# One key block for the plain heads' last 64 queries, and the last 64 tokens' second token product made for two batches at once

## The chip, the core and the metric

The kernel runs on one core of a Trainium2 chip, as one launch. The metric is the device time of that launch in microseconds (us). Three runs of the kernel before the change took 294.07, 294.44 and 294.89 us; the median, 294.44 us, is the time before.

## What is computed

Eight batches of 576 tokens go through attention with 8 heads of 64 channels and then through a mixer. Cut to what matters here:

```python
scores = q @ k.T / sqrt(64)
rel = query_position - key_position
plain  (heads 0..3): keys with 0 <= rel < 32
dilated (heads 4..7): keys with 0 <= rel < 128 and rel % 4 == 0
x = softmax(scores, masked) @ v          # [8, 576, 512], heads side by side
h = relu(x.T @ w_tok1) @ w_tok2          # token mixing: 576 -> 256 -> 576
u = x + h.T
out = u + relu(u @ w_ch1) @ w_ch2        # channel mixing: 512 -> 1536 -> 512
```

A plain head's query sees the 32 keys that end at its own position, so queries 512 to 575 see keys 481 to 575 and no others. A dilated head's query looks back 127 positions.

## The kernel before, in words

**Tokens.** A batch's 576 tokens are four blocks of 128 (`s` = 0 to 3) and a tail of 64 (`s` = 4). Two batches share one 128-row tile for their tails: the even batch has rows 0 to 63, the odd one rows 64 to 127 (`u16t`, `gta[:, :, 512:640]`), so the channel stage does both tails at once, in the odd batch's stage.

**Attention.** Head pairs `hp` 0 and 1 are plain, 2 and 3 dilated. Keys, transposed, are in `kt[hp]`, 640 columns: 0 to 511, then the 64 tail keys, then 64 zeros. Scores are made keys by queries, exponentials go to fp16 tiles (`attp`, `attd`; the tails' to `attt`), and a mask is multiplied in on POOL (`mult`, L112), or, for batches 0 and 1, added on PE as one more matmul per block (`veil`, L390). Batches 0 to 2 make scores with 128-row matmuls (L392); from batch 3 on `scores_twin` (L465 on, matmuls on L475) gives each head of a pair one half of the array's rows. The tail queries of every head are scored against two key blocks, columns 384 to 511 and 512 to 639 of `kt`. `values` (L543 on) multiplies the exponentials with the values `vv` (a column of ones gives the sum): for a plain head seven matmuls for the four blocks (L552, L554) and two for the tail (L562, L564), all of 65 columns. DVE takes the reciprocal (L567) and scales into `xn` (L112).

**Mixer.** `emit_h1` (L570 on) makes the hidden token layer in two column halves and two row halves `jb`, five matmuls each (L576, L578), and a relu moves it to the tile `h1`. `emit_u` (L581 on) multiplies with `w_tok2` and adds `xn` on DVE. For the tail (`s` = 4) it makes the product of 128 weight columns with `h1` (2 matmuls of 512 columns, L601), of which only 64 rows of the result are read: zeros or other tokens' columns fill the rest. For batch 0 the same is written out in `u_half` (L886 on), in halves of 256 columns. `gen_main` (L652 on) is a batch's channel stage: `gp` (L716) and, in odd batches, `gt` (L707) for the tails, then `yp` (L735, and L755 for the tails).

**The order of work.** Instructions run in the order written; `interleave` (L763 on) decides it. It walks through a batch's channel stage (`gen_main(b)`), whose pieces have costs, and puts in a step of the attention and mixing of the following batches as soon as the sum of the costs reaches the step's due time. So stage `b` carries the values and mixing of batch `b+1` (`mix_steps`, L677 on, with due times for the two halves of `h1`, for `u` and for its transposes), and scores, casts, DMA transposes and the copies behind them (`place_steps`, L360 on, on POOL) of batch `b+2`, and loads of batch `b+3`. In steps of stages 2 to 6, `h1` is due at 5.4. Psum banks come from pools: `fl` (three) serves `av`, `h1p`, `up` and, in turn with the others, scores; `sc` has two, `main` three. A bank is written again when its reader is done, and a matmul that needs one waits on the reader's engine.

**Before the first stage** batch 0's attention and mixing run alone, while POOL issues the weight loads in between its casts. POOL then waits for the first channel weights (`gate`, L803) before the loads of batch 1 are let go.

## Time and profile before

| what | value |
|---|---|
| median of the three runs | 294.44 us (294.07 to 294.89) |
| the profiled execution's own span | 293.5 us, 7087 instructions |
| PE, matmul | 279.5 us busy (95%), 2850 matmuls |
| PE, weight load | 214.4 us (73%) |
| DVE | 132.6 us (45%) |
| ACT | 134.4 us (46%) |
| POOL | 165.3 us (56%) |
| granted clock of PE | full in all 40 slices |
| DMA | 52.12 MB, mean 178 GB/s |

The span runs from the first to the last instruction of one profiled execution; a run's time holds about 0.9 us more than it (294.44 - 293.5). An instruction's duration is from its start to its own end. Matmuls are pipelined, so one starts long before the one ahead of it has ended: what a matmul costs PE is the step from its start to the next start, not its duration. L12 is line 12 of the kernel before.

### The profile page before, as it was taken

Reading aid. Unit: us, or ns where it says so; the run is one execution under the profiler, and the core shown is the slowest. Engines: PE = TensorE matmul, PEld = TensorE weight load, DVE = VectorE, ACT = ScalarE, POOL = GpSimd, SP = SyncE. Lnnn points to the kernel's source line nnn. Section 1 sums busy time; section 2 is a strip of 40 time slices with the busy share of each in tenths; the row PEclk is TensorE's granted clock in tenths of the full one; section 3 lists DMA queues with packets and bytes.
Section 4 is the critical chain, followed back from the end, with each engine's and each line's share of the span. In section 5 each row is a group of like instructions: output and inputs, shape, how many; then the busy total and the mean of one; then the engine's idle time right before and its main releaser. Section 6 shows DMA issues by size and latency. Waiting matters only on the chain.

```text
span 293.5 us, 7087 instructions
## 1 busy us (share of the span) xinstructions
PE 279.5 (95%) x2850; PEld 214.4 (73%) x2850; DVE 132.6 (45%) x279; ACT 134.4 (46%) x266; POOL 165.3 (56%) x227
## 2 busy tenths in 40 slices
PE   5899889998999999999999999999999999999994
PEld 2796576796766796689766886698776976896593
DVE  6576658443844218422841246415640264422022
ACT  2774562237554534465346704482346625224500
POOL 5972463225999399929972899369952930000000
PEclk9999999999999999999999999999999999999999
DMA  7998999965899986859995999289874320431032
GB/s 219 269 195 178 288 231 235 256 159 169 271 246 175 308 233 168 123 105 318 254 206 108 304 235 236 56 192 334 211 143 91 93 71 2 88 112 36 2 88 91
DMA packets 103473, 52.12 MB, mean 178 GB/s; under 512 B 71792, under 2 KB 102384, under 8 KB 103440
## 3 DMA queue, kind: packets, MB, share of 16 engines
q1 hardware_dynamic: 99200, 46.55, 64.5%
q0 software_dynamic: 2640, 3.94, 7.6%
q10 hardware_dynamic: 1600, 1.18, 1.3%
q8 instruction: 22, 0.36, 0.5%
q14 instruction: 11, 0.09, 0.1%
HBM read 37.07 MB, written 9.44 MB: 158 GB/s over the span
## 4 chain that ended last, share of the span: by engine, by line
PE 84%; DMA 5%; POOL 3%; DVE 3%; ACT 2%; issue 1%; POOLq 0%; ACTq 0%
PE yp L735 28%; PE gp L716 24%; PE h1p L578 4%; PE up L590 4%; PE yp L755 4%; DMA l_k<-in_k_dram 4%; PE gt L707 3%; PE sc L475 2%; DMA const<-consts 2%; DVE xn L112 1%; PE h1p L576 1%; PE sc L392 1%; POOL vv L102 1%; PE av L559 1%; PE av L554 1%
## 5 line engine op out<-in xcount | busy, mean ns | idle before, releaser
L735 PE MATMUL yp<-w,gt 128*128 128x256 f16 x756 | 86.8, 273 | 0.0
L735 PEld LDWEIGHTS <-gt 128*128 128x128 f16 x768 | 78.5, 106 | 5.9
L106 ACT ACTIVATE gt<-gp 128x512 f16<-128x512 f32 x76 | 45.4, 597 | 81.6 <-PE gp L716 81.1
L716 PEld LDWEIGHTS <-w 128*128 128x128 f16 x384 | 39.1, 114 | 20.0 <-issue 0.5
L112 POOL TENSOR_TENSOR attp<-attp,const 128x1280 f16<-128x1280 f16 x12 | 31.4, 2613 | 38.8 <-ACT attp L499 30.5
L745 DVE TENSOR_TENSOR o<-yp,u 128x512 f32<-128x512 f32 x31 | 21.5, 692 | 63.0 <-PE yp L735 57.7
L716 PE MATMUL gp<-utd,w 128*128 128x512 f16 x120 | 45.5, 380 | 0.0
L716 PE MATMUL gp<-utm,w 128*128 128x512 f16 x120 | 45.5, 379 | 0.0
L716 PE MATMUL gp<-uT,w 128*128 128x512 f16 x144 | 38.4, 379 | 0.0
L112 DVE TENSOR_TENSOR xn<-av,rec 128x320 f16<-128x320 f32 x64 | 31.5, 492 | 2.2
L112 POOL TENSOR_TENSOR attd<-attd,const 128x1024 f16<-128x1024 f16 x12 | 25.3, 2123 | 0.0
L102 POOL CAST c_k<-l_k 128x512 f16<-128x512 f32 x29 | 17.7, 613 | 12.3 <-DMA l_k<-in_k_dram 12.3
L596 DVE TENSOR_TENSOR u<-up,xn 128x512 f16<-128x512 f32 x26 | 18.0, 691 | 8.0 <-PE up L590 7.9
L102 POOL CAST c_q<-l_q 128x512 f16<-128x512 f32 x31 | 18.9, 614 | 4.3 <-DMA l_q<-in_q_dram 4.3
L108 DVE TENSOR_SCALAR gt<-gp 128x512 f16<-128x512 f32 x20 | 13.7, 687 | 11.2 <-PE gp L716 10.8
L106 ACT ACTIVATE h<-h1p 128x256 f16<-128x256 f32 x29 | 11.1, 384 | 15.3 <-PE h1p L578 15.2
L567 DVE RECIPROCAL rec<-av 128x5 f32<-128x5 f32 x64 | 12.1, 190 | 9.4 <-PE av L564 9.0
L392 PEld LDWEIGHTS <-kt 128*128 128x128 f16 x144 | 12.1, 105 | 4.8 <-issue 2.2
L499 ACT ACTIVATE attp<-sc 128x480 f16<-128x480 f32 (+1 forms) x30 | 13.4, 526 | 2.1 <-PE sc L475 2.1
L112 POOL TENSOR_TENSOR attt<-attt,const 128x512 f16<-128x512 f16 (+1 forms) x14 | 14.2, 1016 | 0.0
L605 DVE TENSOR_TENSOR u16t<-up,xn 64x512 f16<-64x512 f32 x7 | 4.8, 690 | 19.8 <-PE up L601 19.8
L499 ACT ACTIVATE attd<-sc 128x512 f16<-128x512 f32 x20 | 10.3, 602 | 6.6 <-PE sc L475 6.6
(136 smaller groups left out, 480.9 us busy)
## 6 DMA issues: line engine op xcount, KB each, us to landing
out_dram<-o SPq DMA_DIRECT2D x72, 128.0 KB, 2.9
l_q<-in_q_dram SPq DMA_DIRECT2D x15, 512.0 KB, 6.1
l_k<-in_k_dram SPq DMA_DIRECT2D x14, 512.0 KB, 6.6
l_vn<-in_v_dram SPq DMA_DIRECT2D x32, 128.0 KB, 6.1
l_vd<-in_v_dram SPq DMA_DIRECT2D x16, 256.0 KB, 4.5
w<-in_moe_w_ch_dram POOLq DMA_DIRECT2D x6, 512.0 KB, 9.5
lt<-in_q_dram SPq DMA_DIRECT2D x8, 128.0 KB, 3.7
l_vt<-in_v_dram SPq DMA_DIRECT2D x8, 128.0 KB, 4.4
```

The costliest lines, as they stand in the source:

```text
L102: eng.tensor_copy(out=out, in_=in_)
L106: nc.scalar.activation(out=out, in_=in_, func=AF.Relu)
L108: eng.tensor_scalar_max(out=out, in0=in_, scalar1=0.0)
L112: eng.tensor_tensor(out=out, in0=x, in1=y, op=ALU.mult)
L392: nc.tensor.matmul(out=out, lhsT=lhsT, rhs=qz[hp][:, h, queries], start=hide is None, stop=True)
L499: nc.scalar.activation(out=out, in_=in_, func=AF.Exp, scale=0.125)
L567: nc.vector.reciprocal(out=rec[:, :, 0], in_=av[:, :, 64])
L578: nc.tensor.matmul(out=p, lhsT=w[:, s, j], rhs=x[:, s, c], start=False, stop=(s == 3))
L596: nc.vector.tensor_tensor(out=u16(b, s), in0=blocks4(p), in1=blocks4(xn[b][:, s]), op=ALU.add)
L716: nc.tensor.matmul(out=p, lhsT=w3_block(cb, mb), rhs=uT[(b, cb)][0], start=(i == 0), stop=(i == 3))
L735: nc.tensor.matmul(out=p[:, c], lhsT=gta[:, mb, a0:m0 + 512:4] if half else gta[:, mb, a0:a0 + 128], rhs=w4[mb][:, c], start=(mb == 0), st ...
L745: nc.vector.tensor_tensor(out=blocks4(o32), in0=blocks4(p), in1=u16(b, s), op=ALU.add)
```

## The change

- **Plain heads, last 64 queries.** Columns 576 to 639 of `kt[0]` and `kt[1]`, which were zeros, now hold a copy of keys 448 to 511 (`transposes` makes it on DVE for batches 0 to 2, `ends` on POOL from batch 3 on). Rows 64 to 127 of `vv[..., 4, 0:4]`, which were zeros, hold the values of the same keys (a second copy in `cast_vn` for `s` = 3, on POOL). So the one block of columns 512 to 639 has all keys that these queries can see. Per plain head one score matmul (with its veil in batches 0 and 1) and one value matmul go; `tails_seen[0]`, the exponential and the mask on POOL of the plain tails are half as wide. Some clears at the start get smaller, one goes, and the table of constants has 608 columns in place of 672.
- **Second token product of the tails.** The even batch's step and batch 0's `u_half(4, ...)` go. In the odd batch's step four matmuls of 64 weight columns and 512 columns write psum rows 0 to 63 (even batch) and 64 to 127 (odd batch), in turns; then come two additions on DVE. Even batches keep `h1` until then (`h1s`).
- **Due time.** In stages 2 to 6 the first half of `h1` is due at 6.2 in place of 5.4.

```diff
 def _np_tails():
...
+    t = 512 + np.arange(64)[None, :]
...
+    for keys, reach, step in ((np.where(p < 64, 512 + p, 384 + p), WINDOW, 1),
+                              (384 + p, WINDOW * DILATION, DILATION), (512 + p, WINDOW * DILATION, DILATION)):
...
     def emit_fixed_late():
         for i in range(2):
-            nc.gpsimd.memset(vv[i][64:128, 4], 0.0)
+            nc.gpsimd.memset(vv[i][64:128, 4, 4:8], 0.0)
...
-        nc.gpsimd.memset(w2a[:, :, S:640], 0.0)
...
     def cast_vn(b, s, eng):
         copy(eng, vv[b % 2][:, s, 0:4, 0:64], l32[(b, "vn")][:, s])
+        if s == 3:
+            copy(eng, vv[b % 2][64:128, 4, 0:4, 0:64], l32[(b, "vn")][64:128, s])
...
             nc.vector.tensor_copy(out=natural(kt[hp][:, 0:512]), in_=main)
+            if hp < 2:
+                nc.vector.tensor_copy(out=kt[hp][:, S:640], in_=kt[hp][:, 448:512])
             return
...
-        return [lambda: plain(0), tails, lambda: plain(1), lambda: dil(2), lambda: dil(3)]
+        def ends():
+            nc.gpsimd.tensor_copy(out=kta[:, 0:2, S:640], in_=kta[:, 0:2, 448:512])
+
+        return [lambda: plain(0), tails, lambda: plain(1), ends, lambda: dil(2), lambda: dil(3)]
...
-            for x in range(2):
-                twin(hp, small, slice(128 * j + 64 * x, 128 * j + 64 * x + 64),
-                     lambda rows: kt[hp][rows, 384 + 128 * x:512 + 128 * x], lambda rows: tta[rows, hp, 0:64])
+            n = 1 + g
+            for x in range(n):
+                c, k0 = 64 * (n * j + x), 384 + 128 * x if g else 512
+                twin(hp, small, slice(c, c + 64), lambda rows: kt[hp][rows, k0:k0 + 128],
+                     lambda rows: tta[rows, hp, 0:64])
...
-        nc.tensor.matmul(out=av[:, 4], lhsT=attt[:, hp, i, c0:c0 + 128],
-                         rhs=va[:, 3, h, :] if hp < 2 else vt[b % 2][:, h - 4, :], start=True, stop=False)
-        nc.tensor.matmul(out=av[:, 4], lhsT=attt[:, hp, i, c0 + 128:c0 + 256], rhs=va[:, 4, h, :],
-                         start=False, stop=True)
+        if hp >= 2:
+            nc.tensor.matmul(out=av[:, 4], lhsT=attt[:, hp, i, c0:c0 + 128], rhs=vt[b % 2][:, h - 4, :],
+                             start=True, stop=False)
+            c0 += 128
+        nc.tensor.matmul(out=av[:, 4], lhsT=attt[:, hp, i, c0:c0 + 128], rhs=va[:, 4, h, :],
+                         start=hp < 2, stop=True)
...
-            odd = b % 2
-            c0 = 448 if odd else 512
             for jb in range(2):
-                nc.tensor.matmul(out=p, lhsT=w2[jb][:, c0:c0 + 128], rhs=h1[jb],
-                                 start=(jb == 0), stop=(jb == 1))
-            rows = slice(64, 128) if odd else slice(0, 64)
-            t = u16t[b // 2]
-            nc.vector.tensor_tensor(out=t[rows], in0=blocks4(p[rows]), in1=blocks4(xn[b][rows, 4]), op=ALU.add)
+                for i in range(2):
+                    nc.tensor.matmul(out=p[64 * i:64 * i + 64], lhsT=w2[jb][:, 512:S], rhs=h1s[b - 1 + i][jb],
+                                     start=(jb == 0), stop=(jb == 1))
+            for i in range(2):
+                rows = slice(64 * i, 64 * i + 64)
+                nc.vector.tensor_tensor(out=u16t[b // 2][rows], in0=blocks4(p[rows]),
+                                        in1=blocks4(xn[b - 1 + i][rows, 4]), op=ALU.add)
...
         for i, s in enumerate((4, 0, 1, 2, 3)):
+            if s == 4 and not b % 2:
+                continue
             steps.append((t_u + du * i, 0.44, lambda s=s: emit_u(b, s, h1)))
...
-    for s in (4, 1, 3):
+    for s in (1, 3):
         u_half(s, 0)
-    for s in (4, 3, 0):
+    for s in (3, 0):
         u_half(s, 1)
...
-                steps += value_steps(b + 1, 0.4, 0.95) + mix_steps(b + 1, 5.4, 9.0, 11.4, 22.4 + late)
+                steps += value_steps(b + 1, 0.4, 0.95) + mix_steps(b + 1, 6.2, 9.0, 11.4, 22.4 + late)
```

On PE, in stage 6 between `gp_8` and `gp_9`, the tail product of batch 7 (`up_4`, from `h_7_0` and `h_7_1`, the two tiles of its `h1`; `w_81` is `w_tok2`) stood like this before:

```order
L716 MATMUL gp_8_4163<-utm_89,w_2_86 128x512
L601 LDWEIGHTS w_81
L601 MATMUL up_4_4169<-h_7_0_3992,w_81 128x512
L601 LDWEIGHTS w_81
L601 MATMUL up_4_4169<-h_7_1_3993,w_81 128x512
L716 LDWEIGHTS w_2_86
L716 MATMUL gp_9_4173<-utd,w_2_86 128x512
```

And at the same place after the change, with batch 6's tiles in it:

```order
L732 MATMUL gp_8_4098<-utm_89,w_2_86 128x512
L614 LDWEIGHTS w_81
L614 MATMUL up_4_4104<-h_6_0_3417,w_81 64x512
L614 LDWEIGHTS w_81
L614 MATMUL up_4_4104<-h_7_0_3931,w_81 64x512
L614 LDWEIGHTS w_81
L614 MATMUL up_4_4104<-h_6_1_3418,w_81 64x512
L614 LDWEIGHTS w_81
L614 MATMUL up_4_4104<-h_7_1_3932,w_81 64x512
L732 LDWEIGHTS w_2_86
L732 MATMUL gp_9_4111<-utd,w_2_86 128x512
```

Two matmuls of 128 rows became four of 64; the two that stood in stage 5 for batch 6 are gone.

On ACT, in stage 5, the relus of the first half of batch 6's `h1` (`h_6_0`, `h_6_1`) and of the channel block `gp_4`, before:

```order
L106 ACTIVATE gt<-gp_3_3547 128x512
L106 ACTIVATE h_6_0_3468<-h1p_0_0_3594 128x256
L106 ACTIVATE h_6_1_3469<-h1p_1_0_3613 128x256
L106 ACTIVATE gt<-gp_4_3631 128x512
L106 ACTIVATE h_6_0_3468<-h1p_0_1_3647 128x256
```

And after:

```order
L107 ACTIVATE gt<-gp_3_3492 128x512
L107 ACTIVATE h_6_0_3417<-h1p_0_0_3553 128x256
L107 ACTIVATE gt<-gp_4_3540 128x512
L107 ACTIVATE h_6_1_3418<-h1p_1_0_3575 128x256
L107 ACTIVATE h_6_0_3417<-h1p_0_1_3592 128x256
```

The two relus of `h1` stand one channel block apart. On PE, between `h1p_0_0` and `h1p_1_0` stood the values of head 6; now the second half of `gp_4` (two matmuls of 512 columns) and the values of head 7 stand there.

On POOL, in stage 4, the last casts, the copies of `place_steps` (`kr` and `tt` are what the DMA transposes bring) and the masks of batch 6, before:

```order
L102 CAST vv_69<-l_vn_2830 128x4x64 x4
L102 CAST vv_69<-l_vt_2833 64x8x64
L102 CAST vv_69<-l_vd_2831 128x4x2x64 x2
L102 CAST vt_71<-l_vx_2832 128x4x64
L366 COPY kt<-kr 128x512
L363 COPY kt<-tt 128x4x64
L366 COPY kt<-kr 128x512
L369 COPY kt<-kr 128x128 x2
L112 TENSOR_TENSOR attp<-attp,const 128x8x160
L112 TENSOR_TENSOR attt<-attt,const 128x4x2x64
```

And after:

```order
L103 CAST vv_69<-l_vn_2788 128x4x64 x4
L103 CAST vv_69<-l_vn_2788 64x4x64
L103 CAST vv_69<-l_vt_2791 64x8x64
L103 CAST vv_69<-l_vd_2789 128x4x2x64 x2
L103 CAST vt_71<-l_vx_2790 128x4x64
L369 COPY kt<-kr 128x512
L366 COPY kt<-tt 128x4x64
L369 COPY kt<-kr 128x512
L376 COPY kt<-kt 128x2x64
L372 COPY kt<-kr 128x128 x2
L113 TENSOR_TENSOR attp<-attp,const 128x8x160
L113 TENSOR_TENSOR attt<-attt,const 128x4x64
```

A cast and a copy came in, and the plain tails' mask has half the elements.

More of the change, by code (lines that the diff above doesn't have):

```diff
@@ L58, in _np_tails @@
     p = np.arange(128)[:, None]
-    j = np.arange(64)[None, :]
+    t = 512 + np.arange(64)[None, :]
     out = []
-    for reach, step in ((WINDOW, 1), (WINDOW * DILATION, DILATION)):
-        for k0 in (384, 512):
-            rel = (512 + j) - (k0 + p)
-            out.append((rel >= 0) & (rel < reach) & (rel % step == 0))
-    return np.stack(out, axis=1).astype(np.float16)
+    for keys, reach, step in ((np.where(p < 64, 512 + p, 384 + p), WINDOW, 1),
+                              (384 + p, WINDOW * DILATION, DILATION), (512 + p, WINDOW * DILATION, DILATION)):
+        rel = t - keys
+        out.append((rel >= 0) & (rel < reach) & (rel % step == 0))
+    return np.concatenate(out, axis=1).astype(np.float16)
 @with_exitstack
@@ L399, in small_bank, with tail_cols @@
         return bank("main", 3, f"sm_{b}_{hp}") if b == 0 else bank("sc", 2, f"sm_{b}_{hp}")
-    def tail_cols(hp, h=None):
-        t = attt[:, hp] if h is None else attt[:, hp, h]
-        return t[..., 64:TW].rearrange("p h (x c) -> p h x c", c=128)[:, :, :, 0:64]
+    def tail_cols(hps, dilated, h=None):
+        t = attt[:, hps, :, 64:TW if dilated else 128].rearrange("p a h c -> p (a h) c") if h is None else \
+            attt[:, hps, h, 64:TW if dilated else 128]
+        return t.rearrange("p z (x c) -> p z x c", c=128)[:, :, :, 0:64] if dilated else \
+            t.rearrange("p z (x c) -> p z x c", x=1)
     def plain_blocks(hp):
@@ L408, in tail_scores @@
     def tail_scores(b, hp, p, c0):
+        n = 1 + hp // 2
         for h in range(2):
-            for x in range(2):
-                c = c0 + 128 * h + 64 * x
-                v0 = BLK + 128 * (hp // 2) + 64 * x
-                score(b, hp, h, p[:, c:c + 64], slice(384 + 128 * x, 512 + 128 * x), slice(512, S),
+            for x in range(n):
+                c = c0 + 64 * (n * h + x)
+                k0 = 384 + 128 * x if n > 1 else 512
+                v0 = BLK + 64 * (x + n - 1)
+                score(b, hp, h, p[:, c:c + 64], slice(k0, k0 + 128), slice(512, S),
                       veil[:, v0:v0 + 64] if veiled(b, hp) else None)
@@ L535, in scores_twin @@
             mask(0)
-        t = attt[:, 2 * g:2 * g + 2].rearrange("p a h c -> p (a h) c")[:, :, 64:TW].rearrange(
-            "p z (x c) -> p z x c", c=128)[:, :, :, 0:64]
+        t = tail_cols(slice(2 * g, 2 * g + 2), g)
         mult(nc.gpsimd, t, t, tails_seen[g])
@@ L677, in mix_steps @@
     def mix_steps(b, t_h1, t_h1b, t_u, t_uT, du=1.0):
-        h1 = [sb.tile([128, DM], FP16, tag="h1", bufs=4, name=f"h1_{b}_{jb}") for jb in range(2)]
+        h1 = h1s[b] = [sb.tile([128, DM], FP16, tag="h1", bufs=4, name=f"h1_{b}_{jb}") for jb in range(2)]
         steps = []
@@ L824 @@
         cast_vn(0, s, nc.gpsimd)
-    nc.gpsimd.dma_start(out=w2a[:, :, 0:S], in_=moe_w_tok2.rearrange("(p j) t -> p j t", j=2))
+    nc.gpsimd.dma_start(out=w2a, in_=moe_w_tok2.rearrange("(p j) t -> p j t", j=2))
     load_w3(0)
@@ L881 @@
         va[h]()
-    h1 = [sb.tile([128, DM], FP16, tag="h1", bufs=4, name=f"h1_0_{jb}") for jb in range(2)]
+    h1 = h1s[0] = [sb.tile([128, DM], FP16, tag="h1", bufs=4, name=f"h1_0_{jb}") for jb in range(2)]
     def u_half(s, half):
@@ L888, in u_half @@
         c = slice(256 * half, 256 * half + 256)
-        rows = slice(0, 64) if s == 4 else slice(0, 128)
-        t = (u16t[0] if s == 4 else u16(0, s))[:, 2 * half:2 * half + 2]
+        t = u16(0, s)[:, 2 * half:2 * half + 2]
         summed = s in (0, 2)
@@ L894, in u_half @@
         for jb in range(2):
-            lhsT = w2p[jb][:, s] if half and s < 4 else w2[jb][:, 128 * s:128 * s + 128]
+            lhsT = w2p[jb][:, s] if half else w2[jb][:, 128 * s:128 * s + 128]
             nc.tensor.matmul(out=p, lhsT=lhsT, rhs=h1[jb][:, c], start=(jb == 0 and not summed),
@@ L900, in u_half @@
         else:
-            nc.vector.tensor_tensor(out=t[rows], in0=blocks4(p[rows]), in1=blocks4(xn[0][rows, s, c]), op=ALU.add)
+            nc.vector.tensor_tensor(out=t, in0=blocks4(p), in1=blocks4(xn[0][:, s, c]), op=ALU.add)
     for jb in range(2):
```

32 lines of the change are left out of this document (16 added, 16 removed).

## The prediction, as put on record before the changed kernel ran

> **What bounds the kernel now.** The page's first part names PE. Busy shares don't say whether its work is the limit, so I next read the busy time by stretches (us from the start of the span; each engine's busy us).
>
> ```profile
> core 0: us, PE busy (x) PEld busy (x) DVE busy (x) ACT busy (x) POOL busy (x), PEclk, DMA share, GB/s
> 0.00:28.00 28.00, 23.43 (x278) 18.52 (x279) 19.05 (x44) 15.45 (x33) 18.38 (x42) 1.00 0.99 210
> ...
> 72.00:98.00 26.00, 25.20 (x269) 17.72 (x268) 14.91 (x35) 12.88 (x25) 24.15 (x37) 1.00 1.00 228
> ...
> 110.00:139.00 29.00, 29.00 (x294) 22.08 (x292) 12.98 (x28) 15.11 (x30) 22.44 (x29) 1.00 0.76 177
> ...
> 202.00:236.00 34.00, 33.71 (x350) 25.61 (x348) 13.88 (x29) 16.36 (x32) 25.20 (x30) 1.00 0.64 154
> ```
>
> Late in the span PE has next to no holes (29.00 of 29.00, 33.71 of 34.00). In the first stretch PE lacks 4.57 us and the DMA engines are full (share 0.99); from 72 to 98 us POOL is full too (24.15 of 26.00). The chain that ended last, read next (start, us, what), says the same of the late part: matmuls back to back.
>
> ```profile
> 252.82 10.48 PE yp L735 x96
> 263.30 3.45 PE gp L716 x16
> ```
>
> A 512-column matmul costs 3.45/16 = 0.216 us there, a 256-column one 10.48/96 = 0.109. So from 98 us on, what PE is spared comes off the span, if its partners keep up; early on the loads decide. I price the two parts apart.
>
> **Part 1: value matmuls of the plain heads' tails.** The step from start to start, stage 5:
>
> ```profile
> 202.32 0.19 PE L562 MATMUL av<-vv,attt 128*128 128x65 f16 x1
> 202.35 0.19 PE L564 MATMUL av<-vv,attt 128*128 128x65 f16 x1
> 202.38 0.39 PE L716 MATMUL gp<-utd,w 128*128 128x512 f16 x1
> ```
>
> 0.03 us each, though one lasts 0.19. Batches 3 to 7, whose values run in the full stages 2 to 6, lose 4 each: 20 x 0.03 = 0.6 us. Those of batches 0 to 2 stand where loads, DVE or POOL decide: 0.
>
> **Part 2: scores of these tails**, batches 3 to 7; tail matmuls are `sc<-tt,kt`:
>
> ```profile
> 222.02 0.38 PE L755 MATMUL yp<-w,gt 128*128 128x512 f16 x1
> 222.33 0.24 PE L475 MATMUL sc<-qt,kt 64*128 64x160 f16 x2
> ...
> 222.81 0.22 PE L475 MATMUL sc<-tt,kt 64*128 64x64 f16 x4
> 222.87 0.22 PE L475 MATMUL sc<-qt,kt 64*128 64x128 f16 x2
> 222.93 0.22 PE L475 MATMUL sc<-tt,kt 64*128 64x64 f16 x4
> 223.08 0.39 PE L755 MATMUL yp<-w,gt 128*128 128x512 f16 x1
> ```
>
> Four take 0.06 us (222.81 to 222.87), two by two on the two row halves. Each four becomes two: 2 x 0.03 = 0.06 a batch, 0.3 in all. The rows price something else: entering the halved array. The `yp` matmul at 222.02 should be followed at 222.24 (+0.216); the scores start at 222.33, so 0.09 lost. The last four should be through at 222.99; `yp` starts at 223.08, 0.09 more. I call it 0.2 us per visit.
>
> **Part 3: the tails' second token product.**
>
> ```profile
> 213.98 0.59 PE L601 MATMUL up<-h,w 128*128 128x512 f16 x2
> 214.41 0.38 PE L716 MATMUL gp<-utd,w 128*128 128x512 f16 x1
> ```
>
> One batch costs 0.43 us. The pairs (2,3), (4,5), (6,7) cost 6 x 0.43 = 2.58. After, a pair has four matmuls of 512 columns. No row of before shows column halves, so I bound them: fully side by side, as the row halves run, 0.43 + 0.2 = 0.63 a pair; one after the other, 0.86 + 0.2 = 1.06; below 0.43 nothing can go, since 512 columns pass twice. I take 0.63, by the nearest row, row halves that share their step: 3 x 0.63 = 1.89, a gain of 0.7 us. Here the weight loads speak against the change:
>
> ```profile
> L601 PEld LDWEIGHTS <-w 128*128 128x128 f16 x14 | 1.2, 98 | 0.7
> ```
>
> A load lasts 98 ns and lies beside the matmul ahead of it; in a pair only the first has none beside it in the new mode, and row halves pay that inside the 0.2. The Trainium skill (TensorEngine Tiling (Array Packing), Restrictions) says that column tiling turns off the fast weight load, and that changing the tiling mode drains the array (Key Properties). The drain agrees with the 0.09 + 0.09 above; no run here shows the slower load. With it (TensorE: Matmul & The Clock Gate, LDWEIGHTS: about one column per 1/1.2 ns, so an estimate of 53 ns for 64 columns) the sum would lose at most 0.2 us over four pairs if one load per pair lay bare.
>
> The two additions now stand together on DVE:
>
> ```profile
> L596 DVE TENSOR_TENSOR u<-up,xn 128x512 f16<-128x512 f32 x26 | 18.0, 691 | 8.0 <-PE up L590 7.9
> ```
>
> Behind the second one wait the four `u` additions and, on SP's queue, the transposes of the tails and of `u`. DVE waited 7.9 us for PE before these 26, 0.3 each, so it makes up the 0.7 us of one more within two or three of them; `up`'s bank of the pool is then free in time. Nothing on the path; if that cover were gone, 0.7 us in each odd batch.
>
> **Part 4: `h1` placed later.** In stage 5 PE stands still between the values of head 6 and `h1p_1_0`, which takes the bank that the relu of `h1p_0_0` on ACT has to free:
>
> ```profile
> 208.04 0.28 PE L559 MATMUL av<-vv,attd 128*128 128x65 f16 x4
> ...
> 208.19 0.19 PE L564 MATMUL av<-vv,attt 128*128 128x65 f16 x1
> 208.68 0.27 PE L576 MATMUL h1p<-xn,w1t 128*128 128x256 f16 x1 [0.29 <-ACT h L106]
> ```
>
> The list of waits counts it (us in total, times, longest):
>
> ```profile
> PE h1p L576 <- ACT h L106: 0.6, 2, 0.3
> ```
>
> From 208.22 to 208.68 it issues nothing: 0.46 us, twice (stages 3 and 5). From the end of `h1p_0_0`'s issue, 208.04, the bank takes 0.64 us. After, two `gp` matmuls (0.43) and head 7's values (0.18) stand between: 0.61. What is late next is still that relu, by 0.03. Gain 2 x 0.43 = 0.9 us; between 0 (the bank is late again) and 0.92. In stages 2, 4 and 6 there was no such stall; the same move is free there.
>
> **Part 5: stage 1.** With batch 2's tail step gone, the channel stage runs ahead and six `yp` matmuls (0.66 us) come between the last transposes, in front of batch 3's scores.
>
> ```profile
> 97.53 0.96 PE L475 MATMUL sc<-qt,kt 64*128 64x160 f16 x14
> 98.31 0.24 PE L475 MATMUL sc<-tt,kt 64*128 64x64 f16 x4
> ```
>
> The same 14 took 0.78 us (97.53 to 98.31) here and 0.48 in stage 5 (222.33 to 222.81, above); the 0.3 was a wait for banks that transposes held. The six cover it: gain 0 to 0.3, I take 0.2.
>
> **Part 6: before 98 us.** Batch 0 saves 4 token products of 256 columns (0.44 us) and some short ones, but then waits for loads that POOL lets go only when the first channel weights have landed:
>
> ```profile
> POOL lt L804 <- DMA w<-in_moe_w_ch_dram: 3.1, 1, 3.1
> ```
>
> So that is worth 0, and DVE's small copies of keys cost 0 behind the same wait (uncovered: two of them, under 0.2 us each by the 0.4 of POOL's larger copy below). The smaller clears and constants let the weight loads go up to 0.4 us sooner, while the DMA engines are full: 0 to 0.4, I take 0.1. Between 38 and 72 us eight score matmuls, with veils and without, go at 0.03: 0.2. Pair (0,1) gains nothing, since batch 0's product was off the path, and pays its visit: 0.2 lost.
>
> POOL is full from 72 to 96 us. Its groups (count, total us, mean ns of one, idle before):
>
> ```profile
> L102 POOL CAST vv<-l_vn 128x256 f16<-128x256 f32 x32 | 11.6, 402 | 0.3 <-DMA l_vn<-in_v_dram 0.3
> L112 POOL TENSOR_TENSOR attt<-attt,const 128x512 f16<-128x512 f16 x10 | 11.6, 1156 | 0.0
> L112 POOL TENSOR_TENSOR attt<-attt,const 128x256 f16<-128x256 f16 x4 | 2.7, 664 | 0.0
> ...
> L363 POOL COPY kt<-tt 128x256 f16<-128x256 f16 x5 | 2.0, 398 | 0.0
> ```
>
> and its last copies for batch 3 in that stretch, in order of time:
>
> ```profile
> 95.42 0.73 POOL L369 COPY kt<-kr 128x128 f16<-128x128 f16 x2
> ```
>
> The added cast has half the partitions of the 402 ns one: at most 0.4 us. A mask of 128 columns: 664 less half of (1156 - 664), about 420 ns, so two of them save 0.5. Before batch 2's values that is 0.1 us less: a gain of 0.1. Then batch 3's cast and key copy (at most 0.4 each) come: POOL would be through at 96.15 + 0.7 = 96.85, and the tail scores of batch 3 that wait for it stood at 98.31. From batch 3 on a batch has 0.3 us more on POOL, in stretches where POOL idles 5 us or more (22.44 of 29.00). No cost. On SP's queue two stores of stage 1 now stand ahead of one load of batch 4, a stage before its use: no cost either. Part 6 sums to 0.1 + 0.2 - 0.2 + 0.1 = 0.2.
>
> **Sum.** 0.6 + 0.3 + 0.7 + 0.9 + 0.2 + 0.2 = 2.9 us. The profiled span of 293.5 becomes 290.6; a run holds about 0.9 more, so the median goes from 294.44 to 291.5.
>
> **Rivals.**
> - *The column halves do not run side by side.* For it: no row shows them, and the two halves take different columns of `h1` from the same 128 partitions. Against: row halves start together. Price: 0.43 for each of four pairs, so a gain of 2.9 - 1.7 = 1.2: 293.2 us. The Trainium skill (TensorE: Matmul & The Clock Gate, Measured speedup) has 2.38 times for three column tiles, which speaks for the forecast.
> - *Weight loads of the halves lie bare.* The four loads of a pair no longer lie beside matmuls, because a load into one half has to wait for the array. By the 98 ns row, at most 4 x 4 x 0.1 = 1.6 of the 2.9: 293.1 us. Against: a halved pass lasts 0.2 us, longer than a load. The rule in the Trainium skill that stands behind it is the one on the fast weight load (TensorEngine Tiling (Array Packing), Restrictions).
> - *Waits take it back.* PE gets to `h1p_1_0`, to POOL's masks before 98 us and to the transposes sooner, and the partners are as late as before: parts 4 to 6 give nothing, a gain of 1.6: 292.8 us. For it: POOL is full there, and 0.61 stands against 0.64.
> - *Slower.* Each change between the two column halves drains the array, as entering a new mode does. Then the 16 half products run alone at 0.216 + 0.2, 6.7 us, where the seven batches on the path had 7 x 0.43 = 3.0; the other parts give 2.4, so 1.3 slower: 295.7 us. It decides from 0.12 us lost per half product on, where the gain is used up. Against: between row halves nothing like it is seen.
>
> **Chances.** Forecast 0.68; halves in turn 0.11; bare loads 0.05; waits 0.12; slower 0.04. A measurement of this kernel can tell about 0.3% from no change, 0.88 us: faster means under 293.56, slower over 295.32, the same what lies between. The forecast is all faster; of the three at 292.8 to 293.2, with some 0.3 us around each, I count 0.20 of 0.28 as faster and 0.08 as the same. So faster 0.88, same 0.08, slower 0.04.
>
> **Range.** The forecast's own bounds: 0.9 could be 0, 0.2 twice could be 0 or 0.3 and 0.5, small terms are rounded: 290.8 to 292.5. To leave out no more than 2 in 10 it must reach the three milder rivals: 290.7 to 293.3.
>
> **What would show it.** In the changed profile: `up` tail matmuls of 64 rows in couples a few ns apart, a pair through in 0.6 us (right), 0.9 or more (halves in turn); steps of 0.2 between the halves with gaps mean draining. No wait of `h1p` for ACT above 0.1 us in stages 3 and 5. 14 score matmuls of stage 1 in about 0.5 us. 2776 matmuls on PE. Wrong would be a PE that has new holes after 98 us, above all before `av` (POOL) or `up` (DVE), or an early part that ends later.

## The result, and the profile after

The changed kernel takes 291.34 us (median; 290.84 to 295.0), the kernel before, run beside it on the same chip, 294.88 us (293.99 to 296.42). The ratio is 0.9894, with a 95% interval of 0.9874 to 0.9914: 2.5 to 3.7 us of 294.4 are gone, 3.1 by the ratio itself. The forecast was 2.9 us, 291.5.

The span of the profiled execution falls from 293.5 to 289.1 us, by more than the medians do. To see where, I take the first gate matmul (`gp`) of every batch as the start of its stage, and the distance to the next as its length (us; the last column ends with the span):

```
                start of 0   stage 0     1      2      3      4      5      6      7    1 to end
before             27.68      43.60   38.58  28.70  34.41  28.70  34.42  27.05  30.37   222.23
after              25.95      43.26   38.10  28.77  33.38  28.77  33.38  27.17  30.36   219.93
forecast           27.6       43.6    37.8   28.7   33.4   28.7   33.4   27.1   30.4   219.5
```

(The last row is worked out of the prediction's terms: each batch's 0.12 for values and 0.06 for scores, 0.43 per product, 0.2 per visit, 0.43 per `h1` stall and so on, laid on the stage in which each stands.) From stage 2 on, all stages came out within 0.1 us of that. Stages 3 and 5 lose 1.03 us each, the even ones take 0.07 to 0.12 longer, and stage 1 loses 0.48 where 0.8 was forecast. What the forecast had not is ahead of stage 1: 71.28 us became 69.21. One part of it is in batch 0's own token mixing. From its first matmul to the first gate matmul, before and then after:

```profile
21.84 0.27 PE L893 MATMUL up<-xn,const 128*128 128x256 f16 x1
...
27.68 2.62 PE L716 MATMUL gp<-uT,w 128*128 128x512 f16 x10
```

```profile
20.77 0.27 PE L908 MATMUL up<-xn,const 128*128 128x256 f16 x1
...
25.95 0.59 PE L732 MATMUL gp<-uT,w 128*128 128x512 f16 x2
```

That is 5.84 us and 5.18, 0.66 less, and neither row of `gp` notes a wait in brackets: PE goes from the mixing straight to the gate. The four products of 256 columns that left this stretch were on the path up to stage 0; whether a later wait for loads takes the gain back is taken up at the end.

The changed profile's answers to the prediction's rows. The page's first part, with the 2776 matmuls named there, and the busy time of the engines over four stretches that match those shown of before:

```profile
PE 275.6 (95%) x2776; PEld 209.2 (72%) x2776; DVE 132.8 (46%) x284; ACT 132.8 (46%) x266; POOL 167.0 (58%) x239
```

```profile
core 0: us, PE busy (x) PEld busy (x) DVE busy (x) ACT busy (x) POOL busy (x), PEclk, DMA share, GB/s
0.00:26.00 26.00, 21.08 (x261) 16.03 (x262) 18.47 (x43) 14.90 (x33) 18.50 (x42) 1.00 1.03 224
70.00:96.00 26.00, 24.98 (x268) 17.83 (x267) 14.32 (x34) 12.69 (x25) 24.82 (x40) 1.00 0.98 229
107.00:136.00 29.00, 29.00 (x289) 21.88 (x287) 13.18 (x28) 14.94 (x30) 23.39 (x31) 1.00 0.70 174
198.00:231.00 33.00, 33.00 (x339) 25.08 (x338) 13.31 (x28) 16.14 (x32) 25.46 (x32) 1.00 0.72 167
```

PE has no hole left in stages 2 and 5 (29.00 of 29.00, 33.00 of 33.00), and POOL is still full in stage 1 (24.82 of 26.00). PE's timeline in stage 2, around the halved product of batches 2 and 3:

```profile
118.35 0.81 PE L732 MATMUL gp<-uT,w 128*128 128x512 f16 x3
119.09 0.62 PE L614 MATMUL up<-h,w 128*64 128x512 f16 x4
119.64 0.62 PE L732 MATMUL gp<-uT,w 128*128 128x512 f16 x2
```

The third `gp` starts at 118.35 + 2 x 0.216 = 118.78, so the product was due at 119.00 and starts 0.09 late. In the trace its four matmuls start at 119.088, 119.091, 119.328 and 119.331: two couples, 3 ns apart inside, so the second couple is through at 119.55. The next `gp` starts 0.09 later. From 119.00 to 119.64 that is 0.65 us, where 0.43 + 0.2 was forecast; the 0.02 more lies between the couples, whose starts are 0.24 apart and not 0.216. The weight loads are not seen on the path although they are slower; their row, min, median and max in ns:

```profile
L614 PEld LDWEIGHTS <-w x16: 106/108/109, 49.9 to 243.4; 128*64 128x64 f16 x16
```

In stage 5, where PE stood still for 0.46 us ahead of `h1p`:

```profile
205.68 0.20 PE L578 MATMUL av<-vv,attt 128*128 128x65 f16 x1
205.73 0.27 PE L590 MATMUL h1p<-xn,w1t 128*128 128x256 f16 x1
```

`h1p` follows 0.05 us behind the last value matmul. The score matmuls of stage 5 and of stage 1, in that order:

```profile
217.90 0.65 PE L485 MATMUL sc<-qt,kt 64*128 64x160 f16 x14
218.39 0.19 PE L485 MATMUL sc<-tt,kt 64*128 64x64 f16 x2
218.41 0.22 PE L485 MATMUL sc<-qt,kt 64*128 64x128 f16 x2
```

```profile
95.82 0.81 PE L485 MATMUL sc<-qt,kt 64*128 64x160 f16 x14
96.46 0.21 PE L485 MATMUL sc<-tt,kt 64*128 64x64 f16 x2
```

The tails' scores of a pair take 0.02 to 0.03 where they took 0.06. The 14 of stage 1 take 0.64 us (0.78 before), not the 0.48 of stage 5 that was forecast: they wait for a bank that a copy on DVE frees now. Last, PE's whole list of waits from 70 us to the end (us in total, times, longest):

```profile
PE av L566 <- POOL attp L113: 0.7, 1, 0.7
PE av L575 <- POOL attt L113: 0.3, 1, 0.3
```

No `h1p` waits for ACT any more; what is left is POOL's masks in stage 1.

### The profile page after: what moved, and what is told of

It reads as the page before. It is cut to its first block, busy times and chain, and to the rows that moved or that the text cites. A ratio compares the mean times of both kernels' runs of the same rounds, so it can differ in the third digit from the quotient of the medians.

```text
span 289.1 us, 6925 instructions
## 1 busy us (share of the span) xinstructions
PE 275.6 (95%) x2776; PEld 209.2 (72%) x2776; DVE 132.8 (46%) x284; ACT 132.8 (46%) x266; POOL 167.0 (58%) x239
## 4 chain that ended last, share of the span: by engine, by line
PE 74%; DMA 12%; POOL 6%; issue 4%; SPq 2%; DVE 1%; ACTq 0%; ACT 0%; POOLq 0%
PE yp L751 25%; PE gp L732 23%; DMA l_k<-in_k_dram 5%; PE h1p L592 4%; PE yp L771 4%; PE up L604 4%; PE gt L723 3%; PE sc L485 2%; DMA lt<-in_k_dram 2%; DMA l_vn<-in_v_dram 2%; DMA l_vt<-in_v_dram 2%; SPq L206 2%; POOL vv L103 2%; POOL attp L113 2%; PE av L571 1%
## 5 line engine op out<-in xcount | busy, mean ns | idle before, releaser
L103 POOL CAST c_q<-l_q 128x512 f16<-128x512 f32 x31 | 19.6, 636 | 4.3 <-DMA l_q<-in_q_dram 2.7
L107 ACT ACTIVATE h<-h1p 128x256 f16<-128x256 f32 x29 | 11.1, 384 | 18.7 <-PE h1p L592 18.3
L103 POOL CAST vv<-l_vn 128x256 f16<-128x256 f32 (+1 forms) x40 | 14.8, 402 | 1.0 <-DMA l_vn<-in_v_dram 0.5
L369 POOL COPY kt<-kr 128x512 f16<-128x512 f16 x10 | 10.7, 1075 | 7.5 <-DMA kr<-c_k 7.5
L398 PEld LDWEIGHTS <-kt 128*128 128x128 f16 x132 | 11.3, 103 | 4.3 <-issue 2.0
```

The costliest lines, as they stand in the source:

```text
L103: eng.tensor_copy(out=out, in_=in_)
L107: nc.scalar.activation(out=out, in_=in_, func=AF.Relu)
```

## The experiments

My theory: the stage part of the gain is the sum of four independent things at their forecast prices (tails 0.9, halved product 0.7, `h1` 0.9, scores of stage 1 a little). Its rivals are those of the prediction. Open was why everything ahead of stage 1 came 2 us earlier. The texts put on record before each run call ACT ScalarE, POOL GpSimd and PE TensorE. All kernels compute the whole reference.

**The old product put back**, for batch 0 too (its edits, and 64 columns of padding for the weights, are not shown):

```diff
...
-            for jb in range(2):
-                for i in range(2):
-                    nc.tensor.matmul(out=p[64 * i:64 * i + 64], lhsT=w2[jb][:, 512:S], rhs=h1s[b - 1 + i][jb],
-                                     start=(jb == 0), stop=(jb == 1))
+            for jb in range(2):
+                nc.tensor.matmul(out=p, lhsT=w2[jb][:, c0:c0 + 128], rhs=h1[jb],
+                                 start=(jb == 0), stop=(jb == 1))
...
```

> The changed kernel with the old second token product of the tails: one product of 128 columns for each batch (two matmuls of 128 x 512), where the change has one pair of halved products for two batches. Theory (the two halves run side by side, so that a pair costs 4 x 0.108 us = 0.43 us and a visit to the halved array 0.2 us, where two batches cost 0.86 us before): from the first gate matmul of one stage to the next, stages 3 and 5 grow from 33.38 to 33.81 us and stage 1 from 38.10 to 38.53, stages 2 and 4 shrink from 28.77 to 28.57 and stage 6 from 27.17 to 26.97; from the start of stage 1 to the end 219.93 becomes 220.6 us (+0.7). First rival (a visit to the halved array eats what the halves save): the same stages move by +0.43 and -0.43, and the end by less than 0.2 us. Second rival (the product also made the later work wait less): the end moves by 1.5 us or more, with a new stall beside the product in the stages that grow.

Measured: stages 1 to 6 took 38.70, 28.52, 33.80, 28.52, 33.81 and 26.93 us, from stage 1 to the end 220.61. Ratio to the kernel before 0.9926 (0.99 to 0.9951). The theory holds to within 0.2 us in each stage, in both directions: the halved product takes 0.43 us off stages 3 and 5, 0.60 off stage 1, and puts 0.25 on each even one. But 0.15 of the 0.60 is not the product: the 14 score matmuls of stage 1 take 0.79 us here (96.99 to 97.78) and 0.64 after the change, the wait for a bank that Part 5 priced. So the product alone is worth 0.53, not 0.68, and a visit costs more than 0.2. From batch 0's first `up` to the first gate matmul it takes 5.84 us here. So it does in both profiles of the kernel before; in the eleven profiles with the new product it is 5.18 or 5.19. The first rival wanted no difference over a pair, the second a new stall; there is neither.

**`h1` at its old place.**

```diff
-mix_steps(b + 1, 6.2, 9.0, 11.4, 22.4 + late)
+mix_steps(b + 1, 5.4, 9.0, 11.4, 22.4 + late)
```

> The changed kernel with the h1 step due at 5.4, as before the change, instead of 6.2. Theory (the two stalls of 0.46 us behind ScalarE in stages 3 and 5 went because h1 comes later, and nothing else moved into their place): the two stalls are back, stages 3 and 5 take 33.8 us each instead of 33.38, the others stay within 0.05 us, and from the start of stage 1 to the end it is 220.8 us instead of 219.93 (+0.9). Rival (they went because the shorter tails moved ScalarE's work ahead, and the due time does nothing): the stages stay within 0.1 us of 33.38 and the end within 0.2 us.

Measured: 28.77, 33.81, 28.77, 33.81, 27.17 for stages 2 to 6, 220.79 from stage 1 to the end; ratio 0.9938 (0.9918 to 0.9959). PE's waits from 70 us on have the old line back, between the two of POOL:

```profile
PE h1p L590 <- ACT h L107: 0.6, 2, 0.3
```

One number in the table of due times is worth 0.86 us, all of it in two stages. The rival (the due time does nothing) is out.

**Without the plain tails' part.** The kernel before, with the new product (its token weights loaded in one piece) and the later `h1` alone; two of its edits:

```diff
...
-mix_steps(b + 1, 5.4, 9.0, 11.4, 22.4 + late)
+mix_steps(b + 1, 6.2, 9.0, 11.4, 22.4 + late)
...
+                for i in range(2):
+                    nc.tensor.matmul(out=p[64 * i:64 * i + 64], lhsT=w2[jb][:, 512:S], rhs=h1s[b - 1 + i][jb],
...
```

> The kernel before with the halved second token product and the later h1, but with the plain heads' last 64 queries seeing two key blocks as before. It computes the whole reference. Theory (the plain tails bring 0.9 us by fewer value and score matmuls, the rest of the gain from stage 1 on is the product's and h1's): stage 2 takes 28.95 us instead of 28.77, stages 3 and 5 33.56 instead of 33.38, stage 6 27.3 instead of 27.17, and from the start of stage 1 to the end it is 220.8 us instead of 219.93 (+0.9). Rival (the fewer matmuls lie beside waits for the masks and exponentials and bring nothing): the stages within 0.05 us of the changed kernel's and the end within 0.3 us.

Measured: stages 2 to 6 took 28.95, 33.54, 28.93, 33.55 and 27.29 us, 0.79 more in all than with the plain tails' part; from stage 1 to the end 220.62 (+0.69); ratio 0.9939 (0.992 to 0.9959). The stages are as expected. The sum is not quite: stage 1 took 38.02 us here and 38.10 with the whole change. There the fewer matmuls bring PE to POOL's masks earlier and it waits for them longer (1.51 us with the whole change, 1.26 here, by the steps of the trace): the rival "waits take it back" is true in this one stage.

**The start of the kernel before** with everything else as changed (the wider constants and the loading of the weights row by row are not shown):

```diff
...
-    w2a = fixed("w2", [128, 2, S])
+    w2a = fixed("w2", [128, 2, 640])
...
-            nc.gpsimd.memset(vv[i][64:128, 4, 4:8], 0.0)
+            nc.gpsimd.memset(vv[i][64:128, 4], 0.0)
+        nc.gpsimd.memset(w2a[:, :, S:640], 0.0)
...
```

> The changed kernel with the start of the kernel before: constants 64 columns wider, the padded token weights loaded row by row into 640 columns with their pad cleared on GpSimd, and the whole clears of the key and value pads. Everything from stage 0 on is as changed. Theory (the smaller start brings the gate weights earlier): the first gate matmul of stage 0 comes 1 to 2 us later than 25.95 us, and the time is 1 us longer. Rival (what the profiled execution showed there, 27.68 us before and 25.95 us after, is scatter of the loads from one execution to the next): the first gate matmul comes within 0.5 us of 25.95 or anywhere between 25.5 and 28, and the time over rounds is within 0.3 us of the changed kernel's.

Measured: first gate matmul at 27.39 us, start of stage 1 at 70.00 (after: 69.21), 219.96 from there to the end; 292.66 us, ratio 0.9931 (0.9907 to 0.9956). That leans to the theory (0.9931 against 0.9894, with intervals that overlap), but the profiled start of stage 1 moved by 0.79 only, and my reason was wrong: the gate weights had landed at the same time (POOL goes on at 22.50 us in both). I wanted to know how much a start scatters.

**Both kernels once more.**

> The changed kernel itself, once more. In the profiled execution of the kernel before, the matmuls between 6.7 and 11.2 us stepped at half rate (128 columns in 107 ns), in that of the changed kernel at full rate from 6.63 us on (55 ns); the other kernels profiled so far went over at 5.4 to 7.4 us. Theory (where it goes over differs from one execution to the next, and the first 2.07 us of the gain in the profiled pair are mostly that and the landing of loads): stages 1 to 6 and the tail again take 219.9 us together within 0.1, while the start of stage 1 moves by some tenths of a us up to 2 us from 69.21. Rival (the changed start itself brings it): the start of stage 1 is again within 0.3 us of 69.21, and all times over rounds lie within 0.5 us of 291.3.

> The kernel before, once more. Theory (half rate up to 11.2 us was one execution's): the matmuls go over to full rate before 8 us this time or at another time than 11.2, and the start of stage 1 comes at 69.5 to 71 us instead of 71.28, with stages 1 to 6 and the tail at 222.2 us together. Rival (the kernel before always starts at half rate): 11.2 us and 71.3 us again.

Measured: the changed kernel 291.71 us (290.61 to 294.26), ratio 0.989 (0.9846 to 0.9935); stage 0 starts at 27.14 and stage 1 at 70.45, 1.24 later than in the first profile, and from there to the end it is 219.94 us, within 0.01. The kernel before: stage 0 at 28.14, stage 1 at 71.75, then 222.27. Its ratio to other runs of itself came out at 0.996 (0.9932 to 0.9987), which shows how far 0.4% can be trusted. PE's first transposes in the two executions of the changed kernel (the first, then the second):

```profile
6.63 0.38 PE L310 MATMUL tp_q<-const,c_q 128*128 128x128 f16 x4 [0.69 <-DMA const<-consts]
6.85 0.39 PE L310 MATMUL tp_k<-const,c_k 128*128 128x128 f16 x4
```

```profile
6.61 0.59 PE L310 MATMUL tp_q<-const,c_q 128*128 128x128 f16 x4 [0.48 <-DMA const<-consts]
6.99 0.63 PE L310 MATMUL tp_k<-const,c_k 128*128 128x128 f16 x4
6.60:11.10 4.50, 3.84 (x32) 3.54 (x32) 1.87 (x5) 2.74 (x5) 4.13 (x14) 1.00 1.15 299
```

Four transposes take 0.22 us in one and 0.38 in the other: PE steps at half rate there, up to 11.0 us, while the granted clock stands at 1.00. So the theory on the changed kernel holds (the stages repeat, the start does not). That on the kernel before falls: it was at half rate up to 11.1 us in both of its executions. From second to second, half rate against half rate, stage 1 starts 1.30 us earlier after the change: 0.34 of it up to batch 0's first `up` (22.30 and 21.96 us), 0.66 from there to the first gate matmul, 0.30 in stage 0. In the first pair, half rate against full, the same three are 1.07, 0.66 and 0.33.

**A longer warm-up**, 12 idle matmuls for 8, to see whether the half rate is what costs:

```diff
-    warm(8)
+    warm(12)
```

> The changed kernel with 12 idle matmuls ahead of the first transposes instead of 8, so that TensorE is kept busy from 2.5 us to the arrival of the constants at 6.6 us. Theory (TensorE goes over to full rate only when it has been busy through most of a stretch of about 3.4 us that starts at no fixed place, and the 8 idle matmuls, 2.5 to 5.9 us, fill such a stretch in some executions only): the profiled execution is at full rate by 8 us at the latest, the first transposes come 0 to 1 us later, and the median over rounds lies 0.3 to 0.8 us under that of the changed kernel run beside other experiments (291.7 us). Rival (what lies between the idle matmuls and 11 us decides, not the idle ones): half rate up to 11 us in some executions as before, the first transposes 0.9 us later there, and the median the same or up to 0.5 us higher.

Measured: full rate from 6.5 us on, first transposes at 7.06, but stage 0 at 27.18 and stage 1 at 70.44, as in the execution at half rate, after a wait of 1.5 us for a cast of batch 1's keys at 33 us; 291.78 us, ratio 0.9909 (0.9878 to 0.9939). Half of each side: the rate is full early here, in this one profile, and it does not help. What PE gained it had lost by 15.1 us, where it stands at the same matmul as in the execution at half rate: from 12.0 us on it waits three times for DVE, 0.40, 0.76 and 0.76 us by the steps, against 0.75 once. That the loads stand behind these waits is not shown. The Trainium skill (TensorE: Matmul & The Clock Gate, Part 1) has the array at half its clock until a window of 3.4 us, which starts at no fixed point, has been busy. The steps of 0.107 us for 128 columns against 0.056 agree, and so does the change from one execution to the next.

**The halves in another order** (both matmuls of one half, then both of the other):

```diff
-            for jb in range(2):
-                for i in range(2):
+            for i in range(2):
+                for jb in range(2):
```

> The changed kernel with the four half products of a pair in another order: both matmuls of the first half of the columns, then both of the second, so that the two middle ones share a half or follow each other in one. Theory (only neighbours in the order that go to different halves run side by side): a pair takes three passes of 0.216 us instead of two, so stages 2, 4 and 6 take 28.98, 28.98 and 27.38 us instead of 28.77, 28.77 and 27.17, stage 0 0.2 us more where it is not waiting, and from the start of stage 1 to the end 220.6 us instead of 219.93 (+0.65). First rival (the hardware finds the free half whatever the order): no change, within 0.1 us. Second rival (a change of half drains the array): 0.3 us or more for each pair on top, 221.5 us or more.

Measured: 28.76, 28.77 and 27.18 us for stages 2, 4 and 6, 219.92 from stage 1 to the end. PE's timeline in stage 2:

```profile
122.02 0.63 PE L614 MATMUL up<-h,w 128*64 128x512 f16 x4
122.58 0.41 PE L732 MATMUL gp<-uT,w 128*128 128x512 f16 x1
```

It lasts 0.63 us where it lasted 0.62, and the next `gp` follows 0.56 us behind its start, where it was 0.55. I expected 0.22 more and was wrong; the first rival holds. The trace has the starts at 122.023, 122.030, 122.263 and 122.270, and the second of these records carries the wait for ACT that only the third and fourth matmul of the program have. So the third one, of the other half, started 0.23 us ahead of the second, which waited for its half. (The median, 292.08, says nothing: the ratio is 0.9899, 0.9856 to 0.9942, and the early part of its profile lost 2.9 us, see the last section.)

**Another bank for batch 2's tail scores.** In the changed kernel PE still waits in stages 0 and 1, and the largest waits from 60 to 96 us are these:

```profile
PE sm L398 <- ACT attp L438: 1.3, 2, 0.8
PE av L566 <- POOL attp L113: 0.7, 1, 0.7
```

```diff
-return bank("main", 3, f"sm_{b}_{hp}") if b == 0 else bank("sc", 2, f"sm_{b}_{hp}")
+return bank("main", 3, f"sm_{b}_{hp}") if b in (0, 2) else bank("sc", 2, f"sm_{b}_{hp}")
```

> The changed kernel with the tails' scores of batch 2 put into the main banks, as those of batch 0 are, instead of the two score banks. Theory (in stage 0, at 66 to 70 us, the tails' scores wait 0.96 and 0.68 us for ScalarE to read a score bank, and behind them the value matmuls wait 1.5 us for GpSimd's masked tails, which are ready no sooner): the two waits of 1.63 us go, the wait for GpSimd grows by about as much, and the start of stage 2 (107.31 us, less what the start of stage 0 differs) moves by less than 0.4 us. Rival (GpSimd was late because the scores were late): the wait for GpSimd stays at 1.5 us or falls, and the time falls by 1.0 to 1.6 us.

Measured: the waits for the score banks are gone, and what is left is one long wait for POOL and a short one for another bank:

```profile
PE av L566 <- POOL attp L113: 1.7, 1, 1.7
PE gp L732 <- DVE o L761: 0.2, 1, 0.2
```

From the start of stage 0 to that of stage 2 it is 82.12 us, 0.76 more than the 81.36 of the changed kernel; 292.22 us, ratio 0.9885 (0.9846 to 0.9923). The theory was half right on the wait: that for POOL did not go, but it grew by 0.36 us only and not by 1.6 (by the steps of the trace PE stood still for 1.87 us, and 0.36 for the other bank, in place of 3.14 in all). Both missed the end: after the long wait PE ran at half rate. The wait and the stretch's row:

```profile
76.76 0.20 PE L566 MATMUL av<-vv,attp 128*128 128x65 f16 x1 [1.71 <-POOL attp L113]
```

```profile
77.90:80.90 3.00, 3.00 (x13) 1.20 (x11) 0.84 (x4) 0.64 (x2) 3.00 (x3) 0.50 1.06 224
```

Three us at half the clock do the work of 1.5, which is more than the 0.9 us of waits saved.

**Batch 2's values cast earlier**, without and with that bank. POOL casts batch 2's values between its masks while it had idled 8 us just before; the first row is the mask of heads 0 and 1, the last that of heads 2 and 3 which PE waits for:

```profile
67.37 2.60 POOL L113 TENSOR_TENSOR attp<-attp,const 128x1280 f16<-128x1280 f16 x1 [8.03 <-ACT attp L447]
...
70.31 1.89 POOL L103 CAST vv<-l_vn 128x256 f16<-128x256 f32 x5
...
74.30 2.61 POOL L113 TENSOR_TENSOR attp<-attp,const 128x1280 f16<-128x1280 f16 x1
```

```diff
-steps += [(19.0, 0.0, start_loads), (24.0, 0.0, lambda: load_v(2))]
+steps += [(19.0, 0.0, start_loads), (20.5, 0.0, lambda: load_v(2))]
...
-steps += at(24.5, 0.5, casts[:9]) + at(34.0, 0.3, casts[9:])
+steps += at(24.5, 0.5, casts[:9]) + at(29.5, 0.3, casts[9:])
```

> The same earlier loading and casting of batch 2's values, with the score banks as in the changed kernel. Theory (the two waits for the score bank stay at 0.96 and 0.68 us, those for the masks, 1.51 us, go): the start of stage 2 comes 79.9 us after that of stage 0, within 0.4, where it was 81.36. Rival (the waits for the masks are set by the late scores): 81 us or more.

> The changed kernel with batch 2's tail scores in the main banks (as in the run with another bank) and with batch 2's values loaded at 20.5 instead of 24.0 and cast on GpSimd at 29.5 instead of 34.0, so that GpSimd casts them in its idle time before the masks. Theory (in the run with another bank the wait only moved to GpSimd's masks, which stood behind 4 us of casts): neither the two score waits of 0.96 and 0.68 us nor the waits for the masks of 1.51 us remain, the start of stage 2 comes 78.6 us after that of stage 0, within 0.5, where it was 81.36, and the time is 2 to 3 us under the changed kernel's. Rival (the masks themselves, 2.6 us each, or ScalarE's exponentials keep the value matmuls late): 80.5 us or more, and the time less than 1 us under.

Measured, start of stage 0 to start of stage 2: 79.94 us with the earlier casts alone (289.69 us, ratio 0.9834, 0.9817 to 0.9852), and 78.63 with the bank as well (289.04 us, ratio 0.9812, 0.9784 to 0.9839). Both are the theory's numbers, 79.9 and 78.6. POOL in the second:

```profile
59.65 1.91 POOL L103 CAST vv<-l_vn 128x256 f16<-128x256 f32 x5
...
67.47 2.61 POOL L113 TENSOR_TENSOR attp<-attp,const 128x1280 f16<-128x1280 f16 x1 [3.58 <-PE yp L751]
70.04 0.42 POOL L113 TENSOR_TENSOR attt<-attt,const 128x128 f16<-128x128 f16 x1
70.43 2.61 POOL L113 TENSOR_TENSOR attp<-attp,const 128x1280 f16<-128x1280 f16 x1
```

The second mask starts 3.9 us sooner, and PE waits for POOL no more in this stretch. This version beats both kernels: by the ratios it is 2.4 us under the changed one.

**The old start again**, on this version:

> The kernel with batch 2's values loaded earlier and its tail scores in the main banks (289.04 us, ratio 0.9812 to the kernel before), with the start of the kernel before (wider constants, token weights loaded row by row into 640 columns, whole clears). Nothing from stage 0 on differs. Theory (the smaller start brings 0.5 to 1 us, as the first run with the old start hinted, 0.9931 against 0.9894): the ratio comes out at 0.983 to 0.985. Rival (the start edits bring nothing and the difference was scatter of the loads): 0.980 to 0.982, with the first gate matmul of stage 0 between 25.9 and 27.4 us, as in the kernels with the new start.

Measured: 290.3 us, ratio 0.984 (0.9814 to 0.9865) against 0.9812; stage 1 starts at 68.85 us against 68.17, the rest is 218.40 and 218.37. So in two pairs the old start was slower by 0.3 to 0.4% (0.8 to 1.1 us), each time with intervals that touch. POOL's opening shows one way how. The cast of the tails' queries (`c_t`), first with the old start, then with the new one, and PE's wait for it with the old start (0.2 us or less with the new one):

```profile
9.45 0.21 POOL L177 MEMSET w<- 128x128 f16 x1
9.61 0.61 POOL L103 CAST c_t<-lt 128x512 f16<-128x512 f32 x1
```

```profile
8.90 0.64 POOL L103 CAST c_t<-lt 128x512 f16<-128x512 f32 x1
```

```profile
PE tp_t L386 <- POOL c_t L103: 0.9, 1, 0.9
```

In all nine profiles with the new start this cast begins at 8.67 to 9.06 us, in all five with the old clears at 9.34 to 9.97. That is systematic, and what it is worth at the end is known only roughly. In the run with `h1` at its old place, whose start is that of the changed kernel, the ratio lies 0.4 us beyond what its stages explain (1.3 against 0.86), which is half of what is at stake here. Nor is this wait in the profiles of the kernel before: at half rate, PE comes to these transposes at 10.8 us in both, when the cast is over (10.58 and 10.09).

## Why the prediction came out

**Parts 1 and 2, the plain tails: right.** 0.9 us were named; 0.79 came back in stages 2 to 6 when this part was undone. The way it was priced, by the step from start to start (0.03 us) and not by the 0.19 us that one matmul lasts, is what made it right. In stage 1 POOL takes 0.08 us of it back, and to the end it is 0.69.

**Part 3, the product: right in kind, 0.2 too large.** 0.63 us a pair was taken from the row halves as the nearest row, and the column halves behave like them: couples 3 ns apart, 0.09 in, 0.09 out. 0.7 us were named. 0.68 came back with the old product, but 0.15 of that is the wait of Part 5; the product alone is worth 0.53. The term that was mis-sized is the visit: 0.22 by the rows and 0.25 by the stages, not 0.2. The rival of halves in turn and that of a drain at each change are out by the couples' starts. The rival of bare weight loads is out too: a load takes 108 ns, longer than the 98 of a whole array's, and still lies beside the other work. The Trainium skill's rule that column tiling turns off the fast weight load (TensorEngine Tiling (Array Packing), Restrictions) fits a load of half the columns that is no shorter; it cost nothing here, since a pass of 0.216 us covers two of them.

**Part 4, `h1`: right.** 0.9 named, 0.86 measured. The margin was as thin as said (0.05 us between `h1p` and the matmul ahead of it, 0.03 named for the relu's), and it held.

**Part 5, the scores of stage 1: too large.** "The six cover it" was wrong: of the 0.3 us, 0.14 went, and it comes back with the old product. The banks that transposes held come free by a copy on DVE now, and it is late as well.

**Part 6, before 98 us: mis-sized, and which of its terms did it stays open.** 0.2 us were named; about 0.8 went by the ratio, once the stages' 2.30 are taken off. Two terms were put at next to nothing.

The first is batch 0's own work, at 0, because PE then waits for loads. Up to stage 0 it gives 0.66 us in every profile with the new product. In stage 0 PE does wait for loads (casts of batch 1's queries and keys, channel weights): by the steps 1.69 and 1.78 us in the two profiles of the kernel before, 1.83 and 1.70 in those of the changed one, 1.2 to 3.1 in the others. So in these pairs the wait did not grow by 0.66, as the prediction has it; but the loads were let go sooner too (POOL goes on at 22.50 and 22.25 us, where it was 24.21 and 22.68), and no run holds them still. Nor does stage 0 show the 0.2 that pair (0,1) was to lose: a wait of 0.46 us of `up` for a relu on DVE, there in both profiles of the kernel before and with the old product, is in none of the others.

The second is "the smaller clears and constants", at 0.1. Two pairs of runs put the whole start at 0.8 to 1.1 us, each with an uncertainty of about the same size, and none of them parts the clears from the constants and the loading. POOL goes on at 22.50 us with the old and the new start, so on the weight loads they do nothing in that pair. They do move a cast of POOL some 0.6 us forward (9.5 to 8.9), and at full rate PE waits for it; that this is what comes through at the end is argued, not shown. The start of stage 1 scatters too much to size either: six profiles of kernels with the changed start and much the same work up to there have it at 69.21, 69.53, 69.88, 70.44, 70.45 and 72.14 us.

**The sum.** Stages 1 to 7 gave 2.30 us where the terms made 2.7; ahead of them about 0.8 went (3.1 - 2.3), where the terms made 0.2. The two errors have opposite signs, and the kernel before came out 0.4 us slower than when the forecast was made (294.88 against 294.44), so that the median lies 0.16 us from the forecast is luck. The forecast's own upper bound was added too low: with 0.9 and both 0.2 at nothing, 1.6 us are left, which is 292.8 and not 292.5; the range as stated covers it. One sentence was beside the point: "a run holds about 0.9 more" than the profiled span. In every run here the time is 1.7 to 1.9 us over that run's own span; by that the profiled execution of before was itself some 0.9 us longer than its median. As only differences were used, nothing hung on it.

Open stays why the kernel before was at half rate up to 11 us in both of its profiles, while of the twelve other profiles only one was, and how much of the gain of the start comes from there: up to batch 0's first `up` the change gains 0.34 us from half rate to half rate, and 1.07 from half to full.

## What to carry to other kernels

Price a short matmul by the step to the next one in the same trace, a visit to a split array by the gaps on both sides of an existing visit, and a stall by asking what stands between; three prices made that way were right to 0.2 us. A term that is put at nothing because of a wait behind it wants the size of that wait on both sides: 0.66 us went ahead of stage 0, and PE's waits for loads behind it were no longer than before. Where loads and a helper engine set the pace, follow the whole queue of that engine: a row of casts that stood between two masks, moved 10 us ahead into POOL's idle time, gave 1.4 us more, and 2.7 with a bank freed. Removing one wait of two in a row can leave much of it in the other (3.14 us became 2.23), and a longer wait can cost the clock.

## What the hardware showed that was not expected

- **A wait of 1.9 us was followed by half the clock in two runs, and one of 2.3 us in a third was not.** In the run with another bank, PE stood still for 1.87 us and 1.1 us later ran at a granted clock of 0.50 for 3.0 us. In the run with the halves in another order two waits for casts (1.16 and 1.89 us by the steps) did the same; PE's list from 26 to 60 us and the stretch behind:

```profile
PE tp_k L310 <- POOL c_k L103: 1.7, 1, 1.7
PE tp_q L310 <- POOL c_q L103: 1.0, 1, 1.0
...
34.00:36.50 2.50, 2.50 (x17) 1.91 (x17) 2.29 (x4) 0.60 (x1) 1.56 (x3) 0.50 1.14 347
```

  In the run with the old product PE stood still for 2.32 us in one piece, and went on at full rate:

```profile
33.23 0.40 PE L311 MATMUL tp_k<-const,c_k 128*128 128x128 f16 x4 [2.16 <-POOL c_k L103]
...
33.20:37.00 3.80, 3.61 (x41) 2.71 (x42) 3.21 (x7) 1.63 (x3) 2.50 (x5) 1.00 1.18 318
```

  Waits of 1.23, 1.37, 1.45 and 1.50 us in four other profiles had no such sequel either. So the length of the wait alone does not decide, and no run here shows what does. The Trainium skill (TensorE: Matmul & The Clock Gate, Part 1) states an idle window of about 3.4 us for this; here 1.87 us in one piece were enough in one run.
- **Matmuls on the two column halves need not alternate in the program.** A matmul for the free half started 0.23 us ahead of an earlier one whose half was busy.
- **At half rate in the opening the profile's granted clock stands at 1.00.** Only the step (0.107 us for 128 columns, 0.056 later) shows it.
